# Attention plus gated feed-forward: middle sums kept on a copy in a second bank, and attention visited one product sooner

## The chip, the cores and the metric

The kernel runs on one core of a Trainium2 chip. The metric is the device time of one execution in microseconds (us); the figure for the kernel before is 922.16 us, the median of three runs (922.1 to 922.37). Engines are named as in the profile: PE is TensorE (matmuls and transposes; PEld are its weight loads), DVE is VectorE, ACT is ScalarE, POOL is GpSimd, SP is the engine that issues most transfers.

## The reference

Windowed attention over 8 batches of 8 heads, 576 positions and 64 columns a head, feeds a gated feed-forward layer over 4608 tokens:

```python
scores = scale * q @ k.T                       # only 0 <= i - j < 64 survives the mask
attn = softmax(scores);  x = heads side by side of (attn @ v)     # 4608 x 512
gate = sigmoid(x @ w_gate);  val = x @ w_val                      # 512 -> 1536
return (gate * val) @ w_out                                       # 1536 -> 512
```

## The kernel before

The tokens stand in ten tiles (two of 384 tokens, six of 512, two of 384). The first two tiles go through plain matmuls (`up`, `down`). The other eight are worked as four **pairs** s = 1 to 4, and both feed-forward layers of a pair are done by a seven-product scheme (Strassen-Winograd): the two tiles of a pair are the two column blocks of one operand, halves of the weight are the row blocks, and seven products with their sums take the place of eight. A number is held as two rounded parts, so each product of a weight block with an input block is three matmuls (`three`, L656).

**The loop.** In pair s, for k = 0 to 5 and for each of the seven products n, `product(s, k, n, m)` (L686) runs for m = 0 (gate) and m = 1 (value): two times three matmuls into one PSUM bank. After a product `combine` (L662) takes it out. Each m has three banks, 0, 1 and 2; `PRODUCTS` (L511) says which product goes to which bank. Later products on a bank accumulate on the earlier ones. A quadrant of the result is handed on by `emit`: for m = 0 ACT makes the gate (`gate_table`, L463), for m = 1 DVE multiplies (`gated`, L469). With P1 the first product and U2 the sum of the first two, `combine` of before does this, for each k and m: ACT copies P1 to SBUF (L674); DVE adds P1 to bank 1 to get U2 (L669); after product 3 DVE adds P1 to bank 1 again, and adds bank 2 to that (L698); product 4 is emitted from its bank; products 5 and 6 each take one DVE add (L698). That is 1 ACT copy and 5 DVE adds. After the six k the **down** products run in the same scheme, `last_product` (L743) with `emit_out` (L753): for each n six k and two halves q of the output, on weights in `wot`. The operands of a down product are cut from the hidden blocks by `h_part` (L733: sums on DVE, a rounding cast on ACT, the rest on DVE); those of an up product by `x_part` and `x_rest` (L641, L652). The names T1 to T4 and S1 to S4 are the sums of input blocks and of weight blocks; T1 is built on T2 (`operand`, L628).

**Attention in between.** The attention of a later pair is done in **visits** inside the up loops: k = 1 to 5 of pair 1, k = 0 to 3 of pairs 2 and 3, thirteen in all. A visit (`far_visits`, L897, and `stage_s`, L309) does the output matmuls (`ob`) of the two units whose softmax is finished, and the score matmuls (`s`) of the next two units; DVE then finds the row minima (L275), ACT does the exponentials block by block (16 blocks for two units of 512 tokens, L290), and `stage_n` normalizes on DVE or POOL. Outputs go to banks 0, scores to banks 1 and to a further pair of banks (`ps_a`). Between two visits the attention weights are transposed on PE: in pair 1 by `stage_b` (L389), whole 128 x 128 blocks, one unit after product 2 and one after product 4 (`WHOLE`); in pairs 2 and 3 by `by_halves` (L373), 64-row blocks, both units after the first half of product 5, into `ps_a` and banks 0. ACT copies the transposes back (L400, L385).

**What sets the order.** `put(time, rank, function, ...)` writes a list of events by hand; they are traced in order of time. PE keeps that order (`pe`). The other engines' queues are ordered ahead of time by the framework's scheduler, with `tc.issue_after(x)` as extra edges; on the chip every engine runs its own queue in order. In pair 1 the weight sums S1 to S4 are made on the fly (`sums_load`, `sums_make`, `sums_split`, `sums_store`), and those for the down layer by `wo_sums`.

## Time and profile before

| | |
|---|---|
| median of three runs | 922.16 us (922.1 to 922.37) |
| span of the profiled execution, first to last instruction | 919.5 us |
| what the median has beyond that span | 2.7 us |
| PE busy in the span | 907.5 us (99%) |
| DVE, ACT, POOL busy | 679.5 (74%), 476.1 (52%), 129.6 us (14%) |
| granted PE clock in all 40 slices of the span | 0.9 or more of full speed; mean 1.000 |

The profile has no separate time for the profiled execution beside its span, so steps are summed against the span, and the median is taken to lie 2.7 us above it. The span is to be read in stages: a head to about 38 us, the first two tiles to 206.7 us, then four pairs, each with an up loop (PE tile `pr`) and a down loop (PE tile `y`): up from 206.7, 404.0, 597.0 and 784.5 us, down from 346.7, 539.9, 727.4 and 871.9 us.

### The profile page before, as it was taken

The numbers are of one execution on the slowest core, as the hardware profiler recorded it, in microseconds if no ns is written. First come the engines' busy times: TensorE is split into PE (matmuls) and PEld (weight loads), VectorE is DVE, ScalarE is ACT, GpSimd is POOL, SyncE is SP. The second block draws the span as 40 slices with busy tenths as digits, with TensorE's granted clock in tenths as the row PEclk, the third lists the DMA queues.
The fourth block names the chain that finished last, engine by engine and source line by source line (L and its number), as shares of the span: only waits on it lengthen the run. The fifth ranks groups of instructions, "written<-read, shape, count | busy, mean of one in ns | idle before, by whom it ended". The sixth has DMA issues, their size and how long they took to land.

```text
span 919.5 us, 18434 instructions
## 1 busy us (share of the span) xinstructions
PE 907.5 (99%) x6584; PEld 788.6 (86%) x6584; DVE 679.5 (74%) x1689; ACT 476.1 (52%) x1208; POOL 129.6 (14%) x204
## 2 busy tenths in 40 slices
PE   6999999999999999999999999999999999999998
PEld 5899999888888888888888888888888888999998
DVE  7887878578898899947666698656655986565881
ACT  7867858554466677525554355424442454222550
POOL 4200000087653402001111100001110000000000
PEclk9999999999999999999999999999999999999999
DMA  9899999679989967787676665766755558888783
GB/s 338 313 406 354 359 324 358 203 244 338 345 315 331 336 241 264 253 270 243 236 233 218 206 189 193 263 217 227 228 188 172 202 187 254 270 252 251 256 256 107
DMA packets 92107, 240.02 MB, mean 261 GB/s; under 512 B 9968, under 2 KB 20080, under 8 KB 92016
## 3 DMA queue, kind: packets, MB, share of 16 engines
q1 hardware_dynamic: 91728, 238.62, 76.1%
q8 instruction: 52, 0.85, 0.4%
q14 instruction: 39, 0.32, 0.1%
q10 hardware_dynamic: 288, 0.23, 0.1%
HBM read 186.91 MB, written 51.90 MB: 260 GB/s over the span
## 4 chain that ended last, share of the span: by engine, by line
PE 97%; ACT 2%; DMA 0%; DVE 0%; issue 0%; SPq 0%; DVEq 0%; ACTq 0%
PE pr L659 47%; PE y L659 23%; PE ph L457 11%; PE y L498 6%; PE s L242 3%; PE ob L425 2%; PE pp L382 1%; PE oo L425 1%; PE pp L395 1%; ACT p L290 1%; DMA k<-in_kT_dram 0%; ACT pT L400 0%; DVE p L275 0%; SPq L195 0%; ACT w L171 0%
## 5 line engine op out<-in xcount | busy, mean ns | idle before, releaser
L659 PE MATMUL pr<-slots,wt 128*128 128x512 f32 (+1 forms) x1728 | 373.8, 375 | 0.0
L659 PEld LDWEIGHTS pr<-slots,wt 128*128 128x128 f32 x1728 | 315.3, 188 | 49.3 <-issue 1.7
L659 PE MATMUL y<-slots,wot 128*128 128x512 f32 (+1 forms) x1008 | 215.8, 375 | 0.0
L659 PEld LDWEIGHTS y<-slots,wot 128*128 128x128 f32 x1008 | 185.5, 188 | 29.6 <-issue 0.2
L465 ACT ACTIVATE g<-c 128x512 f32<-128x512 f32 (+1 forms) x72 | 43.6, 606 | 156.8 <-DVE c L698 154.5
L737 ACT CAST slots<-h 128x512 fp32r<-128x512 f32 (+1 forms) x144 | 83.7, 595 | 71.7 <-PE y L659 41.7
L290 ACT ACTIVATE p<-p,mn 128x128 f32<-128x128 f32 x288 | 108.0, 391 | 22.9 <-DVE mn L275 22.8
L738 DVE TENSOR_TENSOR slots<-h,slots 128x512 fp32r<-128x512 f32 (+1 forms) x144 | 92.9, 666 | 19.4 <-ACT slots L737 18.9
L457 PE MATMUL ph<-slots,w 128*128 128x384 f32 x576 | 104.7, 337 | 0.0
L457 PEld LDWEIGHTS ph<-slots,w 128*128 128x128 f32 x576 | 100.1, 188 | 2.1 <-DVE w L172 0.3
L305 POOL TENSOR_TENSOR p<-p,rs 128x384 f32<-128x384 f32 (+1 forms) x47 | 43.5, 946 | 346.9 <-DVE rs L298 330.7
L659 PE MATMUL pr<-slots,ws 128*128 128x512 f32 x288 | 68.3, 391 | 0.0
L669 DVE TENSOR_TENSOR c<-pr,p 128x512 f32<-128x512 f32 (+1 forms) x48 | 31.4, 655 | 45.0 <-PE pr L659 44.9
L275 DVE CUSTOM_DVE_ANT_0 p<-s,m 128x128 f32<-128x128 f32 x284 | 62.5, 285 | 1.6 <-PE s L242 1.6
L659 PEld LDWEIGHTS pr<-slots,ws 128*128 128x128 f32 x288 | 53.8, 188 | 11.0
L470 DVE SCALAR_TENSOR_TENSOR h<-g,c 128x512 f32<-128x512 f32 (+1 forms) x72 | 48.7, 676 | 6.1 <-DVE c L698 0.5
L498 PE MATMUL y<-w,slots 128*128 128x512 f32 x216 | 52.7, 396 | 0.0
L669 DVE TENSOR_TENSOR u<-pr,p 128x512 f32<-128x512 f32 (+1 forms) x48 | 31.1, 654 | 27.6 <-PE pr L659 14.8
L649 ACT CAST slots<-xf 128x512 fp32r<-128x512 f32 (+1 forms) x48 | 27.9, 598 | 40.5 <-PE y L659 31.7
L498 PEld LDWEIGHTS y<-w,slots 128*128 128x128 f32 x216 | 39.8, 188 | 8.8 <-issue 0.7
L698 DVE TENSOR_TENSOR c<-pr,p 128x512 f32<-128x512 f32 (+1 forms) x48 | 31.2, 654 | 21.3 <-PE pr L659 21.1
L290 ACT ACTIVATION_READ_ACCUMULATOR p<-p,mn 128x1 f32 x240 | 45.1, 188 | 0.0
(93 smaller groups left out, 980.7 us busy)
## 6 DMA issues: line engine op xcount, KB each, us to landing
wt<-wd SPq DMA_DIRECT2D x144, 512.0 KB, 4.3
wot<-wod SPq DMA_DIRECT2D x84, 512.0 KB, 4.2
v<-in_vB_dram SPq DMA_DIRECT2D x24, 512.0 KB, 5.5
wd<-ws SPq DMA_DIRECT2D x48, 256.0 KB, 4.5
w32d<-w SPq DMA_DIRECT2D x36, 256.0 KB, 5.4
wd<-w SPq DMA_DIRECT2D x36, 256.0 KB, 6.1
out_dram<-yo SPq DMA_DIRECT2D x30, 256.0 KB, 5.0
k<-in_kT_dram SPq DMA_DIRECT2D x24, 288.0 KB, 6.3
```

Of the source, the lines that this page charges most:

```text
L275: nc.vector.tensor_tensor_reduce(out=pt[:, u, :], in0=sc[u], in1=masks[key], op0=ALU.add, op1=ALU.min, scale=-SCALE, scalar=3.0e38, accum_ ...
L290: exp = nc.scalar.activation(pt[:, u, :], pt[:, u, :], AF.Exp, bias=mn[:, u:u + 1], scale=-1.0, **sums)
L305: eng.tensor_mul(out=pt, in0=pt, in1=rs.unsqueeze(2).broadcast_to([P, up2(t), P]))
L457: pe(nc.tensor.matmul(ph, l, r, start=i == 0 and 0 in parts, stop=i == len(prs) - 1 and NP - 1 in parts))
L465: act = nc.scalar.activation(g, c, AF.Tanh)
L470: nc.vector.scalar_tensor_tensor(out=out, in0=g, scalar=1.0, in1=val, op0=ALU.add, op1=ALU.mult)
L498: pe(nc.tensor.matmul(yb[y], l, r, start=first and n == 0, stop=last and n == 2))
L659: pe(nc.tensor.matmul(ps, l, r, start=first and i == 0, stop=last and i == 2, skip_group_check=not check))
L669: marks["plus"] = nc.vector.tensor_add(out=o, in0=ps, in1=a).ins
L698: nc.vector.tensor_add(out=c, in0=in0, in1=in1)
L737: nc.scalar.copy(h2[:, 0, :], src)
L738: lo = nc.vector.tensor_sub(out=h2[:, 1, :], in0=src, in1=h2[:, 0, :].bitcast(F32))
```

## The change

The products of the scheme are put in another order and on other banks. Product 0 (A11 B11) is copied by ACT from bank 0 **into bank 2**, and product 2 (S2 T2) and the later ones on that bank accumulate on this copy, so that U2 and the sums built on it come out of PE's accumulation. Product 1 (S1 T1) is copied by ACT to SBUF (tag `p1`), and the sum on bank 2 after product 2 as well (tag `u`). Products 3 and 6 are emitted straight from their banks; products 4 and 5 take one DVE add each. For each k and m that is 3 ACT copies and 2 DVE adds, in place of 1 and 5. T1 is now needed before T2.

In every k that has a visit the products run in the order 0, 1, 3, 2, 5, 4, 6, and the visit comes ahead of product 6 instead of behind it. The exponentials of the second unit are split: its first half is put as before, its second half is held behind the copies into bank 2 of the next k (`marks["seed"]`), save in the last k of a pair. In pair 1 `by_halves` takes the place of `stage_b`, at the place that pairs 2 and 3 use (after the first half of product 5, which is now the fifth of the order). The times of `wo_sums` and of pair 1's weight loads are moved.

```diff
@@ -327,8 +327,8 @@
                 if i:
                     mn_of[(t, p, h)] = mn
 
-    def far_rest(t, p):
-        for h in range(2):
+    def far_rest(t, p, h, behind):
+        with tc.issue_after(marks["seed"]) if behind else nullcontext():
             for u in range(up2(t)):
                 exponential(t, p, h, u, mn_of[(t, p, h)])
 
@@ -508,8 +508,8 @@
 
 
 
-    PRODUCTS = [("A11", "B11", 0), ("S2", "T2", 1), ("S1", "T1", 2), ("S3", "T3", 1),
-                ("A12", "B21", 0), ("A22", "T4", 1), ("S4", "B22", 2)]
+    PRODUCTS = [("A11", "B11", 0), ("S1", "T1", 1), ("S2", "T2", 2), ("A12", "B21", 0),
+                ("S3", "T3", 2), ("S4", "B22", 1), ("A22", "T4", 2)]
     NPR = len(PRODUCTS)
     N_OF = {w: n for n, (w, _, _) in enumerate(PRODUCTS)}
     wd = [[dr.tile([P, 2, 2, H], F32, name=f"wd_{k}_{n}") for n in range(NPR)] for k in range(NK)]
@@ -558,7 +558,7 @@
         a = sums.pop(("o", k))
         b = room(f"wb_{k}").rearrange("p i (a h) -> p (i a) h", a=2)
         s1, s2, s3, s4 = b[:, 1, :], b[:, 3, :], a[:, 1, :], a[:, 3, :]
-        with tc.issue_after(marks["plus"]) if k else nullcontext():
+        with tc.issue_after(marks["plus"]) if k and "plus" in marks else nullcontext():
             nc.vector.tensor_add(out=s1, in0=a[:, 1, :], in1=a[:, 3, :])
         nc.vector.tensor_sub(out=s2, in0=s1, in1=a[:, 0, :])
         nc.vector.tensor_sub(out=s3, in0=a[:, 0, :], in1=a[:, 1, :])
@@ -606,7 +606,7 @@
         with tc.issue_after(marks["p1"]) if k else nullcontext():
             nc.scalar.copy(w2[:, :, 0, :], sw[:, i:i + 2, :])
         if m:
-            with tc.issue_after(marks["plus"]) if k else nullcontext():
+            with tc.issue_after(marks["plus"]) if k and "plus" in marks else nullcontext():
                 nc.vector.tensor_sub(out=w2[:, :, 1, :], in0=sw[:, i:i + 2, :], in1=w2[:, :, 0, :].bitcast(F32))
         else:
             for e in range(2):
@@ -628,9 +628,8 @@
     def operand(s, src, nm, name):
 
         b11, b12, b21, b22 = src
-        if nm == "T2":
+        if nm == "T1":
             nc.vector.tensor_add(out=b11, in0=b11, in1=b12)
-        elif nm == "T1":
             t1 = mp.tile([P, size(s)], F32, name=name, tag="t", bufs=1)
             nc.vector.tensor_sub(out=t1, in0=b22, in1=b11)
             return t1
@@ -641,7 +640,7 @@
     def x_part(s, n, c):
         src = [xf[(2 * s + b, 2 * a + c)] for a in range(2) for b in range(2)]
         nm = PRODUCTS[n][1]
-        if nm == "T2":
+        if nm == "T1":
             nc.vector.tensor_sub(out=src[1], in0=src[3], in1=src[1])
         src = operand(s, src, nm, f"tx_{s}_{c}")
         x2 = slot(2 * n + c, size(s))
@@ -659,49 +658,51 @@
             pe(nc.tensor.matmul(ps, l, r, start=first and i == 0, stop=last and i == 2,
                                 skip_group_check=not check))
 
-    def combine(s, st, n, nm, emit):
+    def combine(s, st, n, nm, seed, emit):
 
         TT = size(s)
         ps = st[PRODUCTS[n][2]][:, :TT]
 
-        def plus(a, tag, bufs):
-            o = mp.tile([P, TT], F32, name=f"{tag}{n}_{nm}", tag=tag, bufs=bufs)
-            marks["plus"] = nc.vector.tensor_add(out=o, in0=ps, in1=a).ins
+        def kept(tag):
+            o = mp.tile([P, TT], F32, name=f"{tag}{n}_{nm}", tag=tag, bufs=2)
+            marks["p1"] = nc.scalar.copy(o, ps).ins
             return o
 
         if n == 0:
-            st["p1"] = mp.tile([P, TT], F32, name=f"p1_{nm}", tag="p1", bufs=2)
-            marks["p1"] = nc.scalar.copy(st["p1"], ps).ins
+            st[2] = seed()
+            marks["p1"] = marks["seed"] = nc.scalar.copy(st[2][:, :TT], ps).ins
         elif n == 1:
-            st["u2"] = plus(st["p1"], "u", 2)
+            st["m5"] = kept("p1")
+        elif n == 2:
+            st["u2"] = kept("u")
         elif n == 3:
-            emit(1, 1, st[2][:, :TT], plus(st["p1"], "c", CB))
+            emit(0, 0, ps, None)
         elif n == 4:
-            emit(0, 0, ps, None)
+            emit(1, 1, ps, st["m5"])
         elif n == 5:
-            emit(1, 0, ps, st["p1"])
+            emit(0, 1, ps, st["u2"])
         elif n == 6:
-            emit(0, 1, ps, st["u2"])
+            emit(1, 0, ps, None)
 
     def product(s, k, n, m):
         st, b = acc[m], PRODUCTS[n][2]
-        if n < 3:
+        if n < 2:
             st[b] = psum(1 + m, b, f"pr{b}_{m}_{s}_{k}")
         for c in range(2):
-            three(st[b][:, :size(s)], wt[(s, k, m, n)], c, xs[(s, n, c)][0], n < 3 and c == 0, c == 1, n < 3)
+            three(st[b][:, :size(s)], wt[(s, k, m, n)], c, xs[(s, n, c)][0], n < 2 and c == 0, c == 1, n < 2)
 
         def emit(r, b, in0, in1):
             t, j = 2 * s + b, k + r * NK
             c = in0
             if in1 is not None:
                 c = mp.tile([P, size(s)], F32, name=f"c{n}_{m}_{s}_{k}", tag="c", bufs=CB)
-                nc.vector.tensor_add(out=c, in0=in0, in1=in1)
+                marks["plus"] = nc.vector.tensor_add(out=c, in0=in0, in1=in1).ins
             if m == 0:
                 gate_table(t, j, c)
             else:
                 gated(hidden(s, k)[2 * r + b], c, gates.pop((t, j)))
 
-        combine(s, st, n, f"{m}_{s}_{k}", emit)
+        combine(s, st, n, f"{m}_{s}_{k}", lambda: psum(1 + m, 2, f"pr2_{m}_{s}_{k}"), emit)
 
     def hidden(s, k):
         if (s, k) not in ht:
@@ -736,7 +737,7 @@
             h2 = slot(slots_of(s)[n * NK + k], size(s))
             nc.scalar.copy(h2[:, 0, :], src)
             lo = nc.vector.tensor_sub(out=h2[:, 1, :], in0=src, in1=h2[:, 0, :].bitcast(F32))
-        if (n, k) == (1, NK - 1):
+        if (n, k) == (2, NK - 1):
             marks["T2", s] = lo.ins
         hs[(s, n, k)] = h2
 
@@ -744,11 +745,11 @@
         b = PRODUCTS[n][2]
         for q in qs:
             st = acc[q]
-            if n < 3 and k == 0:
+            if n < 2 and k == 0:
                 st[b] = psum(1 + q, b, f"y{b}_{q}_{s}")
-            three(st[b][:, :size(s)], wot[(s, n, k)], q, hs[(s, n, k)], n < 3 and k == 0, k == NK - 1, n < 3)
+            three(st[b][:, :size(s)], wot[(s, n, k)], q, hs[(s, n, k)], n < 2 and k == 0, k == NK - 1, n < 2)
             if k == NK - 1:
-                combine(s, st, n, f"y{q}_{s}", lambda r, bb, in0, in1, q=q: emit_out(s, n, q, r, bb, in0, in1))
+                combine(s, st, n, f"y{q}_{s}", lambda q=q: psum(1 + q, 2, f"y2_{q}_{s}"), lambda r, bb, in0, in1, q=q: emit_out(s, n, q, r, bb, in0, in1))
 
     def emit_out(s, n, q, r, b, in0, in1):
         TT = size(s)
@@ -772,7 +773,6 @@
     DPT = DNT / TB
     NPT = (1.8, 1.1, 1.8)
     NEAR = ((6, 12, 14), (15, 21, 23), (24, 30, 32), (33, 39, 41))
-    WHOLE = (2, 4)
     LOAD_AHEAD = 8
     BEFORE, BEHIND = 0, 12
 
@@ -887,14 +887,15 @@
                 tm = now + 0.2 + 0.6 * (n - X_LATE[0])
             put(tm, 5.5, x_part, 1, n, c)
             put(tm + 0.5, 5.6, x_rest, 1, n, c)
-    for k, tm in enumerate((-20, 10, 30, 50, 70, 90)):
+    for k, tm in enumerate((2, 16, 32, 50, 70, 90)):
         put(now + tm - (14 if k else 8), 7, wo_sums_load, k)
         put(now + tm, 7, wo_sums, k)
 
     GROUPS = [[unit(s, 2 * g + i) for i in range(2)] for s in range(2, NS) for g in range(NP)]
+    ORDER = (0, 1, 3, 2, 5, 4, 6)
     AT = [(1, k) for k in range(1, NK)] + [(s, k) for s in range(2, NS - 1) for k in range(NP)]
 
-    def far_visits(v):
+    def far_visits(v, last):
         nonlocal now
         units, done = GROUPS[v] if v < len(GROUPS) else [], GROUPS[v - 1] if v else []
         if v == 0:
@@ -905,7 +906,8 @@
         for i, x in enumerate(units):
             put(now + 0.1, 8, load_v, *x)
             if i:
-                put(now + visit + 2.8, 6, far_rest, *x)
+                put(now + visit + 2.8, 6, far_rest, *x, 0, False)
+                put(now + visit + (2.8 if last else 3 * PRT + 0.05), 6, far_rest, *x, 1, not last)
             put(now + visit + (4.2, 6.9)[i], 6, stage_n, *x)
         for x in GROUPS[v + 1] if v + 1 < len(GROUPS) else []:
             put(now + 0.1, 7.5, load_qk, *x)
@@ -923,23 +925,20 @@
                     for i, at_cut in zip((0, 2), (-14 + 2 * m, -10 + 2 * m) if k == 0 else (-13 + 1.5 * m, -5 + 1.5 * m)):
                         put(now + at_cut, 7, sums_split, m, k, i)
                         put(now + at_cut + 4, 7, sums_store, m, k, i)
-                for n, d in ((0, -23 if k == 0 else -14), (4, -12 if k == 0 else -2), (5, -9 if k == 0 else -1)):
+                for n, d in ((0, -23 if k == 0 else -14), (3, -14.5 if k == 0 else -6.5), (6, -7 if k == 0 else 1.5)):
                     put(now + d, 7.5, w_load, s, k, n)
-            for n in range(NPR):
+            v = AT.index((s, k)) if (s, k) in AT else -1
+            for i, n in enumerate(range(NPR) if v < 0 else ORDER):
                 if s > 1:
                     put(now - 16, 7.5, w_load, s, k, n)
-                v = AT.index((s, k)) if (s, k) in AT else -1
                 for m in range(2):
                     put(now, 9, product, s, k, n, m)
                     now += PRT
-                    if s > 1 and v > 0 and (n, m) == (5, 0):
+                    if v > 0 and (i, m) == (4, 0):
                         put(now, 6, by_halves, GROUPS[v - 1])
                         now += 1.3
-                if s == 1 and v > 0 and n in WHOLE:
-                    put(now, 6, stage_b, *GROUPS[v - 1][WHOLE.index(n)])
-                    now += 1.0
-                if v >= 0 and n == NPR - 1:
-                    far_visits(v)
+                if v >= 0 and i == 5:
+                    far_visits(v, k == NK - 1)
             put(now + 0.5, 5.2, h_diff, s, k)
             made.append(now)
         t0, at_down = now, []
```

## Rows read from the trace of the kernel before

**Rows 1.** Page, busy time: engine, us, share of the span, instructions.
```profile
PE 907.5 (99%) x6584; PEld 788.6 (86%) x6584; DVE 679.5 (74%) x1689; ACT 476.1 (52%) x1208; POOL 129.6 (14%) x204
```
**Rows 2.** Page, the chain that ended last, shares by engine.
```profile
PE 97%; ACT 2%; DMA 0%; DVE 0%; issue 0%; SPq 0%; DVEq 0%; ACTq 0%
```
**Rows 3.** Waits of PE: waiting tile and line, releaser, us, times, longest.
```profile
PE pp L395 <- POOL p L305: 1.9, 4, 0.8
```
**Rows 4.** The chain in order of time (start, us, what): up loop of pair 1.
```profile
206.68 38.08 PE pr L659 x168
...
244.76 1.91 PE s L242 x64
...
255.10 0.87 PE pp L395 x8
255.97 5.46 PE pr L659 x24
...
344.77 1.91 PE s L242 x64
```
**Rows 5.** The same chain: up loop of pair 2.
```profile
426.45 1.91 PE s L242 x64
...
443.55 1.14 PE pp L382 x32
444.69 4.30 PE pr L659 x18
448.99 2.02 PE ob L425 x64
...
475.57 1.91 PE s L242 x64
```
**Rows 6.** The same chain: down loops of pairs 1 and 2.
```profile
346.67 57.35 PE y L659 x252
...
539.92 57.12 PE y L659 x252
```
**Rows 7.** Busy us by stretch (length, PE, PEld, DVE, ACT, POOL, clock, DMA, GB/s): two visits' periods.
```profile
246.70:271.70 25.00, 25.00 (x229) 21.00 (x229) 24.67 (x69) 16.50 (x51) 15.13 (x28) 1.00 0.91 318
...
428.35:452.90 24.55, 24.55 (x246) 20.36 (x245) 16.36 (x55) 13.48 (x46) 4.08 (x4) 1.00 0.70 241
```
**Rows 8.** Groups by line (operation, tiles, shape, count, busy us, mean ns, idle before).
```profile
L674 ACT COPY p<-pr 128x512 f32<-128x512 f32 x36 | 20.3, 577 | 9.0 <-PE pr L659 8.8
L290 ACT ACTIVATE p<-p,mn 128x128 f32<-128x128 f32 x288 | 108.0, 391 | 22.9 <-DVE mn L275 22.8
L698 DVE TENSOR_TENSOR c<-pr,c 128x512 f32<-128x512 f32 x36 | 24.8, 689 | 0.9
```
**Rows 9.** Timeline of ACT after a visit of pair 1 (start, us, instruction).
```profile
248.09 0.40 ACT L290 ACTIVATE p<-p,mn 128x128 f32<-128x128 f32 x1 [1.66 <-DVE mn L275]
...
253.12 0.56 ACT L674 COPY p<-pr 128x512 f32<-128x512 f32 x1
...
254.75 0.56 ACT L674 COPY p<-pr 128x512 f32<-128x512 f32 x1
255.22 1.14 ACT L607 CAST ws<-sw 128x512 fp32r<-128x512 f32 x2
```
**Rows 10.** Timeline of ACT around a visit of pair 2.
```profile
444.85 2.03 ACT L385 COPY p<-pp 128x512 f32<-128x512 f32 x4
...
452.87 0.40 ACT L290 ACTIVATE p<-p,mn 128x128 f32<-128x128 f32 x1 [1.21 <-DVE mn L275]
...
458.29 0.56 ACT L674 COPY p<-pr 128x512 f32<-128x512 f32 x1
...
459.53 0.57 ACT L674 COPY p<-pr 128x512 f32<-128x512 f32 x1
```
**Rows 11.** Timeline of DVE in the down loop of pair 1: the sixth T1 operand.
```profile
367.67 0.68 DVE L738 TENSOR_TENSOR slots<-th,slots 128x512 fp32r<-128x512 f32 x1
```
**Rows 12.** Timeline at the end of the span: the last adds.
```profile
915.67 0.62 DVE L762 TENSOR_TENSOR yo<-y,u_y 128x192 f32<-128x192 f32 x2 [2.57 <-PE y L659]
```

## The prediction

> **What bounds the kernel now.** I read the busy line first [rows 1]: PE is busy 99% of the span. A busy share alone says little, so next the chain that ended last [rows 2]: 97% of it is PE, and no other engine has more than 2%. Then PE's waits: the one row that looks like a wait on transposes (1.9 us in four waits, [rows 3]) names line 395 released by POOL. The transposes of pair 1 wait for a normalization on DVE, not POOL, so this row belongs to the head, which the change doesn't touch. I count on no gain there.
>
> Last, the chain in order of time. In the first two k of pair 1, 168 matmuls take 38.08 us [rows 4], 0.2267 us each, and 252 of the down loop of pair 2 take 57.12 us [rows 6], again 0.2267. PE runs at one pace, at the full granted clock (1.00, its 2.4 GHz level, in both stretches of [rows 7]), and waits for nobody. So all that DVE gives back is worth nothing by itself; only two things count: fewer or cheaper instructions on PE, and new waits of PE. One product (n, m) is six matmuls, 1.36 us; this is the unit for all slack below.
>
> **What the change does to PE's work.** The count of product matmuls stays: seven products, six matmuls for each m. The visits keep their matmuls and are only moved, from behind product 6 to ahead of it; the number of changes between products and attention is the same in pairs 2 and 3. The one piece that PE does in another way is the transposing in pair 1, in four visits (the first visit has nothing to transpose).
>
> - From visit to visit in pair 1: scores begin at 244.76 and at 344.77 us, four periods apart [rows 4], so 25.00 us. In pair 2, with `by_halves` and the same tile sizes: 426.45 to 475.57, two periods [rows 5], so 24.56 us. Difference 0.44 us; by four, 1.77 us.
> - By pieces: `stage_b` is 0.87 us a unit, and the 24 matmuls behind it take 5.46 us where 24 x 0.2267 is 5.44 [rows 4]; two units, 1.78. `by_halves` is 1.14 us for both units, but the 18 matmuls behind it take 4.30 where 18 x 0.2267 is 4.08 [rows 5], so 0.22 us of restart; 1.36. Difference 0.42 us, by four 1.68. I take the periods, since they hold everything between two visits, and keep 1.68 as the lower end.
>
> The restart is where a rule speaks against this part. The row first: PE loses 0.22 us behind the 64-row transposes and 0.02 behind the whole ones. The Trainium skill, TensorEngine Tiling (Array Packing), section Key Properties, says that going from one tiling mode to another drains the TensorE; whole 128-row transposes stay in the products' mode, halves do not. By this the gain of halves is less than their spans tell: by spans alone it would be 1.78 - 1.14 = 0.64 us a visit. The trace agrees with the rule.
>
> **What moves off DVE and onto ACT.** For each k and m three DVE adds go (0.689 us each, [rows 8]) and two ACT copies come (0.577 us each). In a visit's period of pair 1, DVE's 24.67 us of 25.00 fall by 6 x 0.689 = 4.1, and ACT's 16.50 rise by 4 x 0.577 = 2.3 to 18.8 [rows 7]. Both fit in 24.56; in pair 2 they have more room. DVE's part is worth 0, since PE waits for it nowhere. ACT's part costs 0 so long as each copy comes in time. Its cover is the slack until PE writes the bank that was read, or adds to the bank that was filled:
>
> - The copy of product 0 into bank 2 (seed). In a k without a visit PE adds to it with product 2: three products later, 4.08 us. In a k with a visit it is read by product 2 later still, but product 3 comes third and writes bank 0, from which the seed is taken: again three products, 4.08 us. Of before the like copy had seven products before bank 0 was written. It is the tightest of the new waits.
> - How late could it be? In the kernel before, in pair 2, the scores of the middle visit begin halfway between 426.45 and 475.57 us and take 1.91 [rows 5], so they end at 452.9. The copies of product 0 run at 458.29 and 459.53 [rows 10], 5.4 and 6.6 us later, because the scheduler put exponentials first. After the change products 6, 0 and 1, six of 1.36 us, lie between the scores and product 3, so the seeds are due 8.2 us (m = 0) and 9.5 us (m = 1) after the scores' end. Even at the old place, with a gate more ahead of them (0.6 us) and the copy itself (0.57), they would end at 6.6 and 7.8 us: 1.6 us to spare. And the hold on the second half of the second unit's exponentials takes four blocks (4 x 0.391) from in front of them. So no wait in pairs 2 and 3.
> - In pair 1 the scores end at 244.76 + 1.91 = 246.67 us [rows 4], and the copies ran at 253.12 and 254.75 [rows 9], 6.5 and 8.1 us later; with a gate and the copy itself 7.6 and 9.3 against 8.2 and 9.5. That would barely fit, but the exponentials began 1.4 us late there (248.09) behind a full DVE, which the change relieves, and four blocks go behind the seeds. I take 0; the upper end is the two casts of weight sums (1.14 us, [rows 9]) put in front.
> - Seeds of m = 1 also wait for DVE's reading of bank 2 behind product 6. Queued behind a waiting seed on ACT are the held exponentials, and on them the normalization, due 11 products (15 us) later. 0.
> - The copy of bank 2 after product 2 is due before product 4 writes it: three products. The adds behind product 4 are due before product 6: one product and the visit (1.36 + 2.02 + 1.91 us). 0.
>
> **The transposes' copies in pair 1.** Four ACT copies (2.03 us, [rows 10]) have to be done before the outputs (`ob`) begin: in pair 2 they ended at 446.88 and the outputs began at 448.99 [rows 5], 2.1 us to spare. In pair 1 up to four casts of 0.6 us of weight sums may stand in that queue: 2.4 us. So between 0 and 0.3 us, or up to all of the 0.44 if a gate is late too. I take 0, by the row of pair 2, since pair 1's queue is 77% full (18.8 of 24.56).
>
> **The down loops.** T1 is made at n = 1 in place of n = 2. Of before, its last operand in pair 1 was done at 368.35 [rows 11]; PE wanted it at 346.67 + 2 x 8.2 + 6.8 = 369.8, so 1.5 us of slack. It is now due 8.2 us sooner behind the loop's start, but the T2 operands (six splits, 6 x 0.69 = 4.1 us) go behind it, DVE has dropped 4.1 us in the last k, and the visit with its row minima lies 2.72 us further ahead. These are 10.9 us against 8.2: 0, with an upper end in the rivals.
>
> **One answer.** `wo_sums` and the weight loads moved on SP's and POOL's queues: they are read only in the down loop or seven products later; 0. The last piece: ACT copies two pieces of 192 columns instead of DVE's adds, 0.62 us for both [rows 12]; by the mean rows (577 against 689 at 512 columns) at most 0.1 us less; 0.
>
> Sum: 922.16 - 1.77 = 920.39, so **920.4 us**. (Span 919.5 to 917.7; the 2.7 us outside stay.)
>
> **The rivals.**
>
> - *The gain is lost where it is made.* The copies of the transposes in pair 1 come late by about 0.44 us for each of four visits and PE waits ahead of `ob`. For: ACT has 18.8 us of work in 24.56 there, with casts in between. Against: 2.1 us to spare in pair 2. Time 922.2, no change. Chance 0.15.
> - *Slower: seeds too late.* If in pair 1 VectorE still starts the exponentials 1.4 us late and ACT has twelve of them (4.7 us), a gate (0.6) and four casts of weight sums (2.3) ahead of the first seed (0.57), the seed ends 9.6 us after the scores against 8.2, 1.4 us late in each of four k: 5.6 us, so 926.0. There are eleven visits with a next k behind them in the same pair; it decides from 1.77 / 11 = 0.16 us a visit, and makes the kernel slower by 0.2% from (1.77 + 1.84) / 11 = 0.33 us. Chance 0.13.
> - *Slower: VectorE sets the start of the down loops.* If DVE keeps T1 at its old place, 21.7 us behind the loop's start, against 15.0 wanted, PE waits most of 6 us in pair 1 alone. Against it: the queue follows the order of the code, which now has T1 first. With a third of that, 2 us, in each of three loops: 926.4. Chance 0.06.
> - *More is gained: the restart isn't paid.* Then 0.64 us a visit, 2.56 in all, 919.6. Only if the 0.22 us belongs to something else than the halves; pair 2 shows it each time. Chance 0.10.
>
> **How the numbers follow.** A measurement of this kernel tells about 0.2%, 1.84 us, from no change: faster means below 920.32, slower above 924.0. The forecast (chance 0.56) lies on that edge, 920.2 to 920.7 with the tail's 0.1 us and some tenths of waits; I put two fifths of it below the edge. Faster: 0.22 + 0.10 = 0.32. Same: 0.34 + 0.15 = 0.49. Slower: 0.13 + 0.06 = 0.19. The range takes in the forecast, the greater gain and the lost gain with a waiting `ob` (up to 0.6 us more): 919.5 to 922.8. The two slower cases, 0.19, are left out.
>
> **What would show it.** Right: the chain's periods of pair 1 are 24.56 us like those of pair 2, `pp` pieces of 1.14 at both; pairs 2 to 4 keep their periods (24.56) and down loops (57.1); PE's waits name no ACT copy. Wrong: a gap ahead of product 3 or 2 released by ACT's copy (seeds), ahead of `ob` released by line 385, or a `y` piece longer than 57.4 us released by DVE. The forecast is wrong as a whole if PE's pace of 0.2267 us a matmul changes, since everything rests on it.

## The result: 932.06 us, and the profile after

The changed kernel takes 932.06 us (median of four runs, 931.68 to 933.13) beside 922.13 for the kernel before on the same chip: a ratio of 1.0111, with a 95% interval of 1.0097 to 1.0125. The forecast was 920.4 with a range up to 922.8, so it missed by 11.7 us, on the wrong side. The profiled execution took 931.89 us, 930.1 of it span.

The page's busy times and the chain's shares by engine, of the kernel after; they answer to [rows 1] and [rows 2]:

```profile
PE 909.9 (98%) x6648; PEld 788.2 (85%) x6648; DVE 582.8 (63%) x1520; ACT 539.7 (58%) x1329; POOL 130.5 (14%) x204
...
PE 90%; DMA 4%; ACT 3%; DVE 1%; POOL 1%; issue 1%; SPq 0%; ACTq 0%; POOLq 0%
```

DVE gave back 97 us and ACT took on 64, as described. But the chain, 97% PE of before, now spends a tenth of the span off PE (more than PE's idle time, since where PE waits the chain is followed back through the engines that released it). Where PE waits, by PE's waits of the kernel after (waiting tile and line, releaser, us, times, longest):

```profile
PE ob L425 <- ACT p L385: 4.3, 1, 4.3
...
PE pr L658 <- ACT u L668: 2.2, 1, 2.2
PE pr L658 <- ACT pr L673: 2.1, 1, 2.1
...
PE pr L658 <- DMA wt<-wd: 0.5, 1, 0.5
```

None of these four is among PE's waits of before. Together they are 9.1 us, three of the four released by ACT, an engine that is 58% busy. Where in time they lie is read from the chain after, whose pieces answer to [rows 4 to 6]: up loop and down loop of pair 1, then pair 2:

```profile
206.50 20.13 PE pr L658 x89
...
322.27 4.30 PE pr L658 x18
326.58 2.02 PE ob L425 x64
328.59 1.91 PE s L242 x64
...
353.15 1.91 PE s L242 x64
...
358.01 57.12 PE y L658 x252
...
434.83 1.91 PE s L242 x64
...
459.39 1.91 PE s L242 x64
```

Pair 1's up loop runs from 206.50 to 358.01, 151.5 us, where before it took 346.67 - 206.68 = 140.0 [rows 4, 6]: 11.5 us more. The whole loss lies there; the span grew by 10.6, since head, first down loop and end give some tenths back each. Pairs 2 to 4 keep their pace (459.39 - 434.83 = 24.56), the down loop takes 57.12. And the one period of pair 1 in which nothing waits is what was forecast: 353.15 - 328.59 = 24.56, against 25.00 of before.

The 11.5 us are waits and slow starts behind them. PE's timeline of the kernel after at the four waits (start, us, what; in brackets the wait ahead of it), and below it stretches (length, then busy us of PE, PEld, DVE, ACT, POOL, the granted clock, DMA share, GB/s):

```profile
231.51 3.00 PE L658 MATMUL pr<-slots,wt 128*128 128x512 f32 x12 [0.53 <-DMA wt<-wd]
...
266.05 1.65 PE L658 MATMUL pr<-slots,ws 128*128 128x512 f32 x6 [2.16 <-ACT u L668]
...
272.02 3.43 PE L425 MATMUL ob<-p,v 128*64 128x64 f32 x64 [4.32 <-ACT p L385]
...
312.44 4.60 PE L658 MATMUL pr<-slots,wt 128*128 128x512 f32 x12 [2.14 <-ACT pr L673]
```
```profile
272.00:274.00 2.00, 1.98 (x37) 1.98 (x39) 1.95 (x3) 1.59 (x4) 2.00 (x5) 0.50 0.91 334
312.40:314.40 2.00, 1.96 (x5) 1.59 (x6) 1.04 (x2) 0.87 (x3) 2.00 (x4) 0.54 1.04 398
```

The 64 output matmuls behind the wait of 4.32 us take 3.43 us where the undisturbed ones take 2.02: the granted clock of that stretch is 0.50, the 1.2 GHz level. The 12 behind the wait of 2.14 take 4.60 against 12 x 0.2267 = 2.72. With 0.3 at each of the two short ones, the slow starts add 1.4 + 1.9 + 0.3 + 0.3 = 3.9 us. So 9.1 + 3.9 - 1.77 (the gain, which is there) = 11.2 of the 11.5; the first down loop takes 57.12 in place of 57.35 us, so 0.2 of the rest has only moved out of it.

**What the copies stood behind.** ACT's timeline of the kernel after, ahead of the waits at 266.05 and 272.02, and then of the one at 312.44:

```profile
264.89 0.62 ACT L569 CAST wb<-wb 128x512 fp32r<-128x512 f32 x1 [6.32 <-DVE wb L563]
265.42 0.58 ACT L668 COPY u<-pr 128x512 f32<-128x512 f32 x1
268.85 0.62 ACT L607 CAST ws<-sw 128x512 fp32r<-128x512 f32 x1 [2.85 <-POOL sw L595]
...
270.43 2.02 ACT L385 COPY p<-pp 128x512 f32<-128x512 f32 x4
```
```profile
304.67 0.62 ACT L569 CAST wb<-wb 128x512 fp32r<-128x512 f32 x1 [4.03 <-DVE wb L563]
...
306.69 0.40 ACT L290 ACTIVATE p<-p,mn 128x128 f32<-128x128 f32 x1
...
311.81 0.58 ACT L673 COPY pr<-pr 128x512 f32<-128x512 f32 x1
```

In each case ACT stands idle, for 6.32, 2.85 and 4.03 us, at a cast of weight sums: L569 belongs to `wo_sums` (the sums for the down loop), L607 to the weight sums of pair 1. For the waits at 266.05 and 272.02 the copy that PE needs stands right behind such a cast in the same queue, with its own operand there. Those casts wait for sums on DVE and POOL, and these for loads. DVE's and POOL's timelines of the kernel after, and below them DVE's ahead of the wait at 312.44:

```profile
263.98 0.43 DVE L562 TENSOR_TENSOR wb<-wa 128x256 f32<-128x256 f32 x1 [7.06 <-DMA a<-w32d]
```
```profile
265.26 1.46 POOL L593 TENSOR_TENSOR sw<-a 128x128 f32<-128x128 f32 x2 [13.13 <-DMA a<-w32d]
```
```profile
302.57 0.54 DVE L562 TENSOR_TENSOR wb<-wa 128x256 f32<-128x256 f32 x1 [2.13 <-DMA wd<-ws]
...
306.06 0.28 DVE L275 CUSTOM_DVE_ANT_0 p<-s,m 128x128 f32<-128x128 f32 x1
```

The wait at 312.44 is of another kind. Ahead of the seed (311.81, L673) ACT does twelve exponentials and a gate without a pause from 306.69 on, and these need the row minima (L275), which DVE begins at 306.06, 6.1 us after the scores began. DVE had a set of `wo_sums` ahead of them, whose first sum stood 2.13 us for a store. So here the cast's 4.03 us cost little: ACT would have had no row minima before 306 anyway. It is the prediction's rival "seeds too late", once. The experiments bear this out: in the kernel after and its variants below a seed is late behind each visit but pair 1's last whose row minima begin more than 4.2 us after the scores (17 visits, 0.2 to 3.4 us), and behind one other (e8: 4.17 us, 0.2); with the casts of `wo_sums` off ACT (e10) the wait is still 2.10 us, with the minima 6.8 us behind.

For the other two, the loads wait on SP, which issues in order too. SP's queue of the kernel after (L536 stores weight sums, L584 and L552 load the operands of the two kinds of sums), and then of before at the like point:

```profile
237.56 1.23 SPq L584 DMA_DIRECT2D a<-w32d  x2
...
242.00 10.47 SPq L536 DMA_DIRECT2D wd<-ws  x4
...
257.91 0.47 SPq L552 DMA_DIRECT2D wa<-w32d  x1
258.42 0.90 SPq L584 DMA_DIRECT2D a<-w32d  x2
```
```profile
237.44 0.94 SPq L584 DMA_DIRECT2D a<-w32d  x2
238.42 0.93 SPq L552 DMA_DIRECT2D wa<-w32d  x2
239.40 0.43 SPq L584 DMA_DIRECT2D a<-w32d  x1
...
241.51 0.43 SPq L584 DMA_DIRECT2D a<-w32d  x1
```

In before all four loads of pair 1's sums for the next k go out by 241.9 us, ahead of this k's later stores. In after the order is another: two of the four and a load for `wo_sums` stand behind four stores that take 10.47 us in SP, most of it waiting for POOL's splits, and behind the visit's own loads of q and k, and go out at 257.9 to 259.3. POOL's waits for these loads between 206 and 360 us grow from 10.3 us to 38.9:

```profile
POOL sw L593 <- DMA a<-w32d: 10.3, 3, 4.9
```
```profile
POOL sw L593 <- DMA a<-w32d: 38.9, 6, 13.1
```

The first row is of before, the second of after. So the trace shows a chain through five queues: stores wait for POOL, loads behind them in SP, POOL and DVE for the loads, casts on ACT for POOL and DVE, copies behind the casts, PE for the copies.

### The profile page after: what moved, and what is told of

Read it like the earlier page. It is cut to its first block, busy times and chain, and to the rows that moved or that the text cites. A ratio compares the mean times of both kernels' runs of the same rounds, so it can differ in the third digit from the quotient of the medians.

```text
span 930.1 us, 18453 instructions
## 1 busy us (share of the span) xinstructions
PE 909.9 (98%) x6648; PEld 788.2 (85%) x6648; DVE 582.8 (63%) x1520; ACT 539.7 (58%) x1329; POOL 130.5 (14%) x204
## 4 chain that ended last, share of the span: by engine, by line
PE 90%; DMA 4%; ACT 3%; DVE 1%; POOL 1%; issue 1%; SPq 0%; ACTq 0%; POOLq 0%
PE pr L658 43%; PE y L658 23%; PE ph L457 11%; PE y L498 6%; PE s L242 3%; PE ob L425 2%; ACT p L290 2%; PE pp L382 2%; DMA a<-w32d 1%; PE oo L425 1%; DMA wd<-ws 1%; DMA wt<-wd 1%; DMA k<-in_kT_dram 0%; ACT pT L400 0%; POOL sw L593 0%
## 5 line engine op out<-in xcount | busy, mean ns | idle before, releaser
L739 DVE TENSOR_TENSOR slots<-h,slots 128x512 fp32r<-128x512 f32 (+1 forms) x144 | 91.0, 654 | 36.5 <-ACT slots L738 36.1
L470 DVE SCALAR_TENSOR_TENSOR h<-g,pr 128x512 f32<-128x512 f32 (+1 forms) x48 | 31.3, 652 | 103.7 <-PE pr L658 88.9
L275 DVE CUSTOM_DVE_ANT_0 p<-s,m 128x128 f32<-128x128 f32 x284 | 62.5, 286 | 1.4 <-PE s L242 1.2
L699 DVE TENSOR_TENSOR c<-pr,u 128x512 f32<-128x512 f32 (+1 forms) x48 | 31.4, 654 | 41.0 <-PE pr L658 40.2
L465 ACT ACTIVATE g<-c 128x512 f32<-128x512 f32 (+1 forms) x48 | 29.1, 606 | 45.2 <-DVE c L699 45.0
L653 DVE TENSOR_TENSOR slots<-xf,slots 128x512 fp32r<-128x512 f32 (+1 forms) x48 | 32.8, 694 | 20.9 <-ACT slots L648 20.6
L593 POOL TENSOR_TENSOR sw<-a 128x128 f32<-128x128 f32 x24 | 15.9, 680 | 198.7 <-DMA a<-w32d 192.6
```

The lines of the kernel that those rows point to most:

```text
L275: nc.vector.tensor_tensor_reduce(out=pt[:, u, :], in0=sc[u], in1=masks[key], op0=ALU.add, op1=ALU.min, scale=-SCALE, scalar=3.0e38, accum_ ...
L465: act = nc.scalar.activation(g, c, AF.Tanh)
L470: nc.vector.scalar_tensor_tensor(out=out, in0=g, scalar=1.0, in1=val, op0=ALU.add, op1=ALU.mult)
L653: nc.vector.tensor_sub(out=x2[:, 1, :], in0=src, in1=x2[:, 0, :].bitcast(F32))
L699: marks["plus"] = nc.vector.tensor_add(out=c, in0=in0, in1=in1).ins
L739: lo = nc.vector.tensor_sub(out=h2[:, 1, :], in0=src, in1=h2[:, 0, :].bitcast(F32))
```

## The experiments

A trace names what ended a wait, not what would end it if that were gone. Where an interval is given a kernel ran 4 to 11 times; every other time below is a single run, and ten runs of one kernel spread over 2 to 3 us (e11, e15). Losses and gains "of after" are differences of raw times; taken from before on each chip they come out 0.1 to 0.6 us smaller. Three theories compete: the **moved times** of `wo_sums` alone do the harm; the copies **stand in order** behind casts whose sums are late (by loads, by SP's order, or by DVE's queue); or ACT is simply **too full** for copies that are due so soon. The parts were tried from both kernels, the rest from the kernel after.

**The parts alone.** The old times of `wo_sums` in the kernel after, and the new times in the kernel before:

```diff
-    for k, tm in enumerate((2, 16, 32, 50, 70, 90)):      # e1, in after
+    for k, tm in enumerate((-20, 10, 30, 50, 70, 90)):
-    for k, tm in enumerate((-20, 10, 30, 50, 70, 90)):    # e2, in before
+    for k, tm in enumerate((2, 16, 32, 50, 70, 90)):
```

> The changed kernel with the event times of the down layer's weight sums (wo_sums) put back to those of before (-20, 10, 30, 50, 70, 90 in place of 2, 16, 32, 50, 70, 90). Theory A (the moved times made the lateness: their loads, row sums and casts now fall into k = 0 to 2 of pair 1, where SP's queue is already behind): PE's three long waits in pair 1 (2.2, 4.3, 2.1 us) go, span 918 to 920 us, time 920 to 922. Theory B (the casts of pair 1's weight sums are held behind later copies, because the mark p1 now names the copies after products 1 and 2 too): nothing or little changes, 930 to 932. Theory C (ScalarE simply has too much in its queue in pair 1 with two more copies for each k and m): 930 to 932, with waits at other places.

> The kernel before with nothing but the new event times of wo_sums (2, 16, 32, 50, 70, 90). Theory A: the lateness comes without the new scheme too, 925 to 932 us. Theories B and C: 922, within 0.5 us, since the products' slack is as before.

Measured: e1 925.12, e2 922.28 (before: 922.02). In before the new times cost nothing that can be told, and no wait of PE appears there. Not only had its copies seven products of slack: the loads weren't late either (POOL waits 10.1 us for them). In after the old times win back 7 us, but PE then waits 3.2 us at the start of pair 1, behind copies of the first tiles' outputs (`yo`) that stand behind the first set; and POOL still waits 26.3 us for its loads. So the moved times do harm only together with the rest of the change, and aren't all that makes the loads late.

The changed kernel also sets the mark "p1", behind which casts of pair 1's sums are placed, at the copies of products 1 and 2, not only at the first. With the mark at the first alone:

```diff
-            marks["p1"] = nc.scalar.copy(o, ps).ins       # e3, in after; e8: times (2, 10, 30, ...) too
+            nc.scalar.copy(o, ps)
```

> The changed kernel, but the mark p1 is set by the copy of product 0 alone, not by the copies after products 1 and 2, so the casts of pair 1's weight sums are held behind an earlier instruction. Theory B: most of the 11 us comes back, 920 to 923 us, and POOL's splits (line 615) no longer hold up the stores on SP (36 us of waits fall to about 15). Theories A and C: 929 to 932 us.

> The changed kernel with the mark p1 set by the copy of product 0 alone (as in e3, 926.2 us) and wo_sums at 2, 10, 30, 50, 70, 90 (as in e1, 925.1 us, but with the first set left at 2, since at -20 PE waited 3.2 us for a copy out of bank at the start of pair 1). If the two effects are apart they add: 920 to 922 us. If they are one lateness seen from two sides: 924 to 926.

Measured: e3 926.22, e8 929.05. The first wins 6 us (POOL still waits 36.4 us for its loads), and the earlier second and third set on top of it lose 3 again: a wait of 6.2 us at the start of pair 1 takes the place of the others.

```profile
PE pr L658 <- ACT yo L501: 6.2, 1, 6.2
```

This row is of e8, from PE's waits. Small edits of the order don't add up; each makes another queue head stand.

The halves alone, in the kernel before (`by_halves` in pair 1 behind product 5, m = 0, in place of the two `stage_b`), three rounds:

```diff
-                    if s > 1 and v > 0 and (n, m) == (5, 0):     # e4, in before
+                    if v > 0 and (n, m) == (5, 0):
...
-                if s == 1 and v > 0 and n in WHOLE:
-                    put(now, 6, stage_b, *GROUPS[v - 1][WHOLE.index(n)])
-                    now += 1.0
```

> The kernel before with by_halves in pair 1 at the place that pairs 2 and 3 use, and nothing else. The step of the prediction that gave the gain: the periods of pair 1 go from 25.0 to 24.56 us, 1.77 us in four visits, so 920.4 us. If the copies of the transposes come late in pair 1 by themselves, without the new scheme: 922 or more, with PE waiting ahead of the outputs.

Measured: 929.75, ratio 1.0084 (1.0067 to 1.0101). PE's waits of e4:

```profile
PE pp L382 <- DVE h L470: 4.6, 3, 2.8
```

The halves are written into a bank that DVE must have read after product 4 just before, and DVE of before is full there (24.67 of 25.00 us, [rows 7]). So the gain of 0.44 us a visit isn't had by the halves alone. In after DVE has room, and the new order puts product 2 between the product on that bank and the halves; which of the two keeps PE free there, no run separates.

**What the casts wait for.** All from the kernel after: the loads of pair 1's weight sums 8 us sooner for k = 2 to 5 (e5); the later stores on SP put behind the next loads (e6); the casts of `wo_sums` on DVE (e10); and `wo_sums` with its transfers but without its sums and casts (e7).

```diff
-    put(now + make - (6 if k else 4), 7, sums_load, m, k)                              # e5
+    put(now + make - (6 if k < 2 else 14) + (2 if not k else 0), 7, sums_load, m, k)
...
-    put(now + at_cut + 4, 7, sums_store, m, k, i)                                      # e6
+    put(now + at_cut + (4 if k == 0 or k == NK - 1 else 4.5 + 5 * i - 1.5 * m), 7, sums_store, m, k, i)
...
+        with tc.issue_after(marks["sums_load"]):      # around the stores of e6
...
-                nc.scalar.copy(hi.bitcast(F32R), lo)                                   # e10
+                nc.vector.tensor_copy(out=hi.bitcast(F32R), in_=lo)
...
-            nc.vector.tensor_add(out=s1, in0=a[:, 1, :], in1=a[:, 3, :])               # e7
-        nc.vector.tensor_sub(out=s2, in0=s1, in1=a[:, 0, :])
-        nc.vector.tensor_sub(out=s3, in0=a[:, 0, :], in1=a[:, 1, :])
-        nc.vector.tensor_sub(out=s4, in0=a[:, 2, :], in1=s2)
...
-                nc.scalar.copy(hi.bitcast(F32R), lo)
-            nc.vector.tensor_sub(out=lo.bitcast(F32R), in0=lo, in1=hi)
```

> The changed kernel with the loads of pair 1's weight sums (sums_load) issued 8 us earlier for k = 2 to 5, everything else as changed. Theory P (the loads of weight sums stand on SP's queue behind stores that wait for POOL's splits, so the sums are made late, and ScalarE's casts of them stand ahead of the copies that PE waits for): POOL's waits for these loads (39 us in pair 1) shrink to some 10 us as in the kernel before, and with them the 4.3 us wait ahead of the outputs; 921 to 925 us. Theory Q (the waits come from the down layer's sums, wo_sums, whose own loads aren't moved): the two waits of 2.1 to 2.2 us behind wo_sums' casts stay, the one of 4.3 too: 929 to 932. Theory C (ScalarE simply has too much to do in pair 1): 928 to 932, waits at other places.

> The changed kernel with the stores of S3 and S4 (sums_store, k = 1 to 4) put later and held behind the next k's loads on SP's queue, so that no load of weight sums stands behind a store that waits for POOL. Theory P: 920 to 924 us, SP's waits for POOL (36 us) halve, and POOL's waits for loads too. If the loads wait for buffers rather than behind the stores, SP waits at the loads instead and little changes: 928 us or more. Theory C: 928 to 932.

> The changed kernel with wo_sums cut to its transfers: the loads and the stores stay, the sums on DVE and the casts on ScalarE are left out, so the down layer's S weights are not what they should be. Theory Q: the two waits behind wo_sums' casts go (4.3 us and their slow restarts), 923 to 926, the wait ahead of the outputs stays. Theory P: the same or more, since DVE isn't held up 7 us at its first sum either, but POOL's waits for loads stay above 25 us. Theory C: 6 x 2 casts less on ScalarE in pair 1 (0.62 us each) take some of it, 926 to 929.

> The changed kernel with the twelve rounding casts of wo_sums on DVE instead of ScalarE. Theory Q1: ScalarE no longer waits for DVE's sums (12 us in pair 1), PE's two waits of 2.1 to 2.2 us behind those casts go with their slow restarts, 922 to 926 us; the wait ahead of the outputs, behind the cast of pair 1's own sums, may stay. Theory C: about the same, 922 to 926; e9 tells the two apart.

Measured: e5 925.83, e6 923.51, e7 919.69 (before on that chip 921.53), e10 925.18. e7 is the decisive one; what it leaves out is needed, so its output isn't the reference's. The chain of e7, the scores of pair 1's visits:

```profile
242.68 1.91 PE s L242 x64
267.27 1.91 PE s L242 x64
291.83 1.91 PE s L242 x64
316.39 1.91 PE s L242 x64
340.95 1.91 PE s L242 x64
```

Periods of 24.59 and three times 24.56, no wait of PE in pair 1, and 1.84 us faster than before, near the forecast's 1.77. The two times are single runs, and runs of before on one chip lie 1.9 us apart (921.26 to 923.15), so the periods carry this and the time only agrees. The sums and casts of `wo_sums` are thus what the loss hangs on, but e7 doesn't say in which queue: without them pair 1's loads go out sooner too (245.78 and 254.38 where after has 258.42 and 263.19), ACT stands 1.0 us in all for POOL's sums, though POOL still waits 29.8 us for its loads, and the row minima begin 1.9 to 2.2 us behind the scores. Loads sooner (e5) are worth 6.2 us of after's loss, SP's order (e6) 8.6, the casts on DVE 6.9; none alone gives the gain back. In each of the three a seed is late (2.1, 1.1 and 2.1 us at the like place), in e6 a weight load too (2.0).

**Late operands, or a full ACT?** In e13 the sums and casts of `wo_sums` stay, in the same number, but take a constant tile in place of the loaded weights, and none of their results is stored; e9 leaves the stores of the first two sums in.

```diff
+        c = ident.unsqueeze(1).broadcast_to([P, 2, P])             # e9, e13
...
-            nc.vector.tensor_add(out=s1, in0=a[:, 1, :], in1=a[:, 3, :])
+            nc.vector.tensor_add(out=two(s1), in0=c, in1=c)
...
-                nc.sync.dma_start(out=wo_at(k, name), in_=t4[:, 2 * i:2 * i + 2, :])
+                nc.sync.dma_start(out=wo_at(k, name), in_=a[:, 2 * i:2 * i + 2, :])   # e13 alone
```

> The changed kernel with every sum of wo_sums on DVE and every cast on ScalarE kept in number and size, but working on a constant tile, so that none of them waits for a load (the S weights of the down layer are not what they should be; loads and stores stay). Theory Q1 (ScalarE and DVE are not too full; they stand still in order behind sums whose loads are late): pair 1 runs in periods of 24.56 us, 919.5 to 921.5 us. Theory C (the twelve casts are too much for ScalarE beside the new copies): 925 us or more.

> The changed kernel with all sums of wo_sums on DVE and all its casts on ScalarE kept in number and size, on a tile that no load fills and no store reads; loads and stores stay and move the loaded rows, so the S weights of the down layer are not what they should be. Theory Q1 (standing in order behind late sums): pair 1 in periods of 24.56 us but for the wait ahead of the outputs behind POOL's sums, 919.5 to 922 us. Theory C (too much work on ScalarE): 925 us or more, with PE waiting for ScalarE's copies at three places or more.

Measured: e9 928.93, which tells little: in it the casts of the second pair of sums wait for the stores of the first (9.0 us on ACT in five waits), a wait of the edit's own. e13 924.51. ACT's timeline of e13 at the start of pair 1, and PE's right behind:

```profile
206.88 1.14 ACT L609 CAST ws<-sw 128x512 fp32r<-128x512 f32 x2 [3.17 <-POOL sw L597]
209.62 0.62 ACT L609 CAST ws<-sw 128x512 fp32r<-128x512 f32 x1 [1.60 <-POOL sw L601]
...
210.67 1.55 ACT L501 COPY yo<-y 128x512 f32<-128x512 f32 x3
```
```profile
211.30 1.65 PE L660 MATMUL pr<-slots,wt 128*128 128x512 f32 x6 [2.62 <-ACT yo L501]
...
306.47 3.02 PE L660 MATMUL pr<-slots,wt 128*128 128x512 f32 x12 [0.99 <-ACT pr L675]
```

With every cast of `wo_sums` still on ACT, 7.6 of the 12.4 us between e7 and after are gone: a full ACT isn't the main cause. The time lies between the two that were expected, and it isn't late loads alone: the stores no longer wait for casts either. What PE waits for now, 2.62 us at the start of pair 1 where after had no wait, is again behind casts that stand for POOL's sums, ahead of copies that PE wants; the 0.99 is a seed whose row minima began 4.3 us behind the scores. In the undisturbed period of after ACT is busy for 19.91 of 24.56 us, and PE waits for nothing:

```profile
328.59:353.15 24.56, 24.56 (x249) 20.37 (x251) 21.36 (x64) 19.91 (x58) 0.00 (x0) 1.00 0.76 256
```

**Putting it together.** e11 is e6 with e10; e12 has the loads of `wo_sums` 20 us ahead besides, where they were 14; e14 is e12 with the sets at (2, 14, 26, 50, 70, 90); e15 is e14 with the casts on ACT again.

```diff
-        put(now + tm - (14 if k else 8), 7, wo_sums_load, k)       # e12, e14, e15
+        put(now + tm - (20 if k else 8), 7, wo_sums_load, k)
```

> The changed kernel with the casts of wo_sums on DVE (e10) and the stores of S3 and S4 behind the next k's loads on SP's queue (e6, 923.5 us). If the two causes of late copies on ScalarE are the late loads of both kinds of weight sums, nothing is left in front of PE: 919.5 to 921.5 us, faster than both kernels; 922 to 924 if the wait for a weight load of 2.0 us seen in e6 stays.

> As e11, with the loads of wo_sums 20 instead of 14 us ahead of its sums. If the sums on DVE still wait for their loads in e11 and PE feels it, 0.5 to 2 us faster than e11; if not, the same within 0.5 us.

> e12 (stores behind loads on SP, casts of wo_sums on DVE, its loads 20 us ahead; 922.1 us) with its second and third set at 14 and 26 in place of 16 and 32, so that none lies on DVE ahead of the first visit's row minima. If that set made PE's last wait: the wait of 1.4 us and its restart of 0.3 go, 920.0 to 920.8 us, 0.1 to 0.2% faster than before. If not, 922.

> As e14, with the casts of wo_sums on ScalarE as in the changed kernel. If ScalarE only stood behind late sums, and these come in time now: as e14, 920 to 921 us. If the casts are too much for it in pair 1: 922 to 925 us.

Measured: e11 921.93, ratio 0.9998 (0.9988 to 1.0007); e12 922.06; e14 920.58, ratio 0.9988 (0.9979 to 0.9997); e15 922.94, ratio 1.0009 (1.0000 to 1.0018). In e11, which was to leave no wait, two seeds are still late (1.5 and 0.2 us), with the row minima 5.8 and 4.3 us behind the scores. In e12 one wait is left in pair 1. PE's waits of e12, and DVE's timeline ahead of it:

```profile
PE pr L659 <- ACT pr L674: 1.4, 1, 1.4
```
```profile
246.85 0.95 DVE L570 TENSOR_TENSOR wb<-wb 128x512 fp32r<-128x512 f32 x1
...
248.59 0.28 DVE L275 CUSTOM_DVE_ANT_0 p<-s,m 128x128 f32<-128x128 f32 x1
```

A set of `wo_sums` stands on DVE ahead of the row minima (L275), so the exponentials start late and the seed, behind them on ACT, is late too: the prediction's "seeds too late", 1.4 us, once. In e14 the sets lie elsewhere, and PE's waits are 0.8 and 0.5 us. It is 1.45 us by medians below before, 0.12% by the ratio: the best of the kernels that leave nothing out, and hardly more than its interval. e15's runs lie in two groups, five at 921.3 to 922.1 and five at 923.8 to 924.3. Its profiled run, of the first group, has a wait of 1.8 us released by `yo` at the start of pair 1, where ACT stood 2.35 us at the first set's cast; no seed is late in it, with every cast on ACT. What makes the second group wasn't seen in a profile.

## Why the prediction was wrong

**Right.** The gain: 24.56 us a period in pair 1 wherever nothing waits (after, e7, e14), 1.84 us in all in e7, which can't be told from the 1.77, and 0.22 us of restart behind the halves (4.30 for 18 matmuls, also in pair 1). The trace agrees with the rule of the Trainium skill that a change of tiling mode drains the TensorE (TensorEngine Tiling (Array Packing), section Key Properties), now in pair 1 too. Pairs 2 and 3, T1 and the down loops (57.12) came as forecast: no wait of PE there. From the start of the last copies to the end of the span lie 3.4 us, where from the start of the last adds it was 3.8 (926.72 of 930.1 in after, 915.67 of 919.5 in [rows 12]): 0.4 us less, some tenths more than the 0.1 allowed. Two of the signs that were named for being wrong came: gaps ahead of product 3 released by ACT's copy and ahead of `ob` released by line 385.

**Wrong, the main step: "One answer".** `wo_sums` and the weight loads on SP's and POOL's queues were put at 0, because their results are read much later. That holds for the results. It doesn't for what stands behind the instructions: the casts of both kinds of sums are on ACT, ahead of the copies, and they wait for loads which stand behind stores on SP; the sums themselves stand on DVE ahead of the row minima. Put at 0, `wo_sums` measured 12.4 us in the kernel after (e7, without the sums and casts); with its old times 6.9 (e1), with SP's order mended 8.6 (e6), with the casts no longer behind loads 7.6 (e13) are won back. These overlap and aren't to be added. The mark "p1" on the later copies, which holds casts of pair 1 back, wasn't priced at all: with it at the first copy alone 5.8 us come back (e3).

**Wrong, "ACT's part costs 0 so long as each copy comes in time".** The slack was counted well: three products in place of seven. But the queue ahead of each copy was measured by the durations of [rows 9], as if everything in it could run at once. It put two casts ahead of a seed at 1.14 us as the upper end; a cast ahead of a copy stood up to 6.32 us. And 77% busy, the argument that pair 1's queue has room, is no argument: it was 81% full in the undisturbed period (19.91 of 24.56), without a wait.

**Wrong, the rivals' sizes.** Two rivals named the places, the seeds of pair 1 and the outputs behind the transposes' copies, but as the same delay in each of four visits (1.4 and 0.44 us), by a DVE that starts late and by ACT's fill. What came was 4.3 us once, by casts that stood for late sums, and 2.1 us once. For the seed the rival had the mechanism right, as the twelve exponentials and the gate show; the forecast took 0 because the change relieves DVE, but the sets of `wo_sums` filled the place: the row minima began 6.1 us behind the scores at 299.94, where in before they took 2.5 to 3.2 in the first three visits. The copy of product 2 (2.2 us at 266.05), put at 0 with "three products", was named by none.

**Left out: the slow start.** Each wait was priced at its length. The four waits of 9.1 us cost 13.0.

What stays open is how the loss divides between SP's order, the loads' landing and DVE's own queue: each repair moves the head at which ACT stands. Open too is why pair 1's loads go out late in after and not in e2: neither the old times nor the mark alone brings POOL's waits for them back to 10 us.

## What to carry to other kernels

Where a change takes slack from copies on an engine that issues in order, busy shares don't tell whether they come in time. List what stands ahead of each tightened copy in its queue, and for each of these what it waits for, queue by queue, down to a load; an instruction whose result nobody needs soon can still hold up the one behind it. And moved times alone can be harmless in the old kernel (e2) and costly in the new one, so try a moved part in both.

## What the runs showed of the hardware

A wait of PE costs more than its length, and not always by the same. Behind 2.14 us of waiting in after, 12 matmuls took 4.60 us, at a granted clock of 0.54 in the next 2 us (shown above). Behind 2.10 us in e10 the same 12 took 3.03, at 1.00. PE's timeline of e10 and its stretch:

```profile
307.17 3.03 PE L658 MATMUL pr<-slots,wt 128*128 128x512 f32 x12 [2.10 <-ACT pr L673]
```
```profile
307.15:309.15 2.00, 1.98 (x9) 1.63 (x10) 1.50 (x3) 1.88 (x8) 2.00 (x4) 1.00 1.05 399
```

In both, PE had run products at full clock until the wait. The wait's length doesn't decide: behind 2.05 us in e5 the same 12 took 4.61, behind 3.25 us in e1 PE ran on at a granted clock of 1.00. What does, no run here shows. At the full clock stopping and starting costs 0.3 us beside the wait (3.03 - 2.72), also with a short one (0.53 us of waiting, 3.00).
